# Attention value products in plain float32 for all batches, and four units of block 1 among block 0's output layer

## The chip, the core and the metric

The kernel runs on one core of one Trainium2 chip. A core has a matrix engine (TensorE, PE in the profile; PEld is its weight load), a vector engine (VectorE, DVE), a scalar engine (ScalarE, ACT), GpSimd (POOL) and a queue engine (SyncE, SP) that issues most of the DMAs. The metric is device time of the whole program in microseconds (us), less is better.

## What is computed

Three layers follow each other. The first is attention over 8 batches, 8 heads, 576 tokens and head size 64, with keys and values averaged over groups of 8 tokens, so that each query sees 72 keys:

```
k_p = k.reshape(B, H, Sp, pool, D).mean(axis=3)      # Sp = 72
v_p = v.reshape(B, H, Sp, pool, D).mean(axis=3)
attn = softmax(q @ k_p^T / sqrt(D))
x = attn @ v_p                                       # to 4608 tokens x 512
h = max(max(x @ w1, x @ w2), x @ w3)                 # 512 -> 768
y = h @ w_out                                        # 768 -> 512
out = square(max(y @ w_in2, 0)) @ w_out2             # 512 -> 2048 -> 512
```

All inputs and outputs are float32. The weights come as 64-bit numbers and are converted on the chip.

## The kernel before

The 4608 tokens are taken in 12 blocks of 384. A batch has 576 tokens, so it gives one piece of 384 and one of 192 to the blocks. For each block there are first the attention pieces, then 22 steps on PE: 18 groups of twelve matmuls for the three products x @ w1, w2, w3 (`ps` at L513; six units `f`, three experts each), and 4 groups of eighteen matmuls for the output layer (`ps` at L532). Results of the blocks go to DRAM (`y_dram`), and after all blocks a second part of the program (`moe2_in`, `moe2_out`) does the last layer.

Products of the two MoE layers need float32 accuracy. Each operand is split into a high part in the type fp32r and the remainder, also fp32r (`split`, `split_to` at L133 and L134: a copy on ACT that rounds, a subtraction on DVE or POOL), and three of the four partial products are summed in PSUM (`PARTS`). The alternative is a matmul on plain float32 tiles.

An attention unit (`attend`) is one pair of heads (p of 4) in one piece. It has: `load` (DMAs of k, q, v), `prepare` (pooled k into `kbd`), `softmax` (pooled v into `vst`, scores `sc` at L353, row maximum, exponentials, sums, division on POOL), `transpose` (probabilities `ss` into `tr` in PSUM and from there into `pt` in SBUF) and `values` (the products of `pt` with `vst`, into `x`, which is then an operand of L513). For batch 0 (`whole`, b < NATURAL) `pt` and the pooled values `vst_f` are plain float32 tiles, the two heads are summed into one PSUM bank `av` by two matmuls (L398), and `x` is split from that bank. For batches 1 to 7, `pt` is split into high and low part (L384, L385), `vst` too (L209, L210), each head has its own bank (`av0`, `av1`) and two matmuls (L409, L410) that leave the parts in two halves of the bank's rows; these are summed through `xf` (a copy on ACT, L412, and an addition on DVE, L413), and `x` is split from `xf`.

The order is made in two steps. Every piece of work gets a time in steps (`todo`, sorted in `run`): block j's matmul groups stand at j * 22 and after, attention for a block a number of steps ahead of it (LEAD and LAG numbers), the loads of weights at the start. Then a scheduler of the compiler moves instructions within engines by its own simulation. For block 1, the first `AHEAD` units (three groups each) are put among the four groups of block 0's output layer, at equal distances; their `h` tiles lie in a pool of their own, `ah_p`, since block 0 still holds the six tiles of `h_p`. In the opening, the 18 weight tiles of w1, w2, w3 and then the six of w_out (`wo1`) are loaded (`load_raw`), converted (two instructions each on ACT and DVE, `convert`) and split (ACT and POOL, L133 and L134). Their raw form lies in four buffers that they share with the loads of k and v (`place`).

Of the kernel before, what the change touches and what calls it, by code (L numbers as in the profile page):

```python
# [20 lines left out]
P = 128  # L21
# [42 lines left out]
AHEAD = 2  # L64
# [18 lines left out]
def as_f32(ap):  # L83
    return ap.bitcast(F32)
# [8 lines left out]
def attention_moe_kernel(ctx: ExitStack, tc: tile.TileContext, q, k, v, vn, w1, w2, w3, wo1, wi2, wo2, out):  # L93
# [95 lines left out]
    xf_p = s_at.enter_context(tc.tile_pool(name="xf_p", bufs=1, side="right"))  # L189
# [6 lines left out]
    vst = kv_p.tile([SP, NPAIR, 4, D], F32R, name="vst")  # L196

    kbd = kv_p.tile([P, NPAIR, 2, SP], F32, name="kbd")
    nc.gpsimd.memset(kbd, 0.0)
    vst_f = []  # L200
    for _ in range(2):
        vf = t_p.tile([P, T1], F32, tag="ys", name="vst_f")[:SP].rearrange("s (p a d) -> s p a d", a=3, d=D)
        nc.gpsimd.memset(vf, 0.0)
        vst_f.append(vf)
    K_SCALE = 1.0 / (POOL * D**0.5)
    V_SCALE = 1.0 / POOL

    def split_scaled(hi, lo, src, scale):
        nc.scalar.activation(hi, src, AF.Copy, scale=scale)  # L209
        nc.vector.scalar_tensor_tensor(  # L210
            out=lo, in0=src, scalar=scale, in1=as_f32(hi), op0=ALU.mult, op1=ALU.subtract
        )
# [27 lines left out]
    def prepare_v(p, vr):  # L240
        vs = sm_p.tile([SP, 2, D], F32, tag="vs", name="vs", bufs=2)
        nc.vector.tensor_reduce(out=vs, in_=vr, axis=AX.X, op=ALU.add)
        split_scaled(vst[:, p, 0:4:3], vst[:, p, 1:3], vs, V_SCALE)
# [14 lines left out]
    def pool_v(tiles):  # L258
# [8 lines left out]
        for h in range(2):  # L267
            vh = vp.rearrange("s (p h d) -> s h p d", h=2, d=D)[:, h]
            for i in range(2):
                nc.scalar.activation(vst_f[i][:, :, 2 * h], vh[:, 2 * i : 2 * i + 2], AF.Copy, scale=V_SCALE)  # L270
# [48 lines left out]
    def attend(j, b, s0, n, p, t):  # L319

        kr, vr, qr, pt, sms = [], [], [], [], []
        first, whole = s0 == 0, b < NATURAL
# [47 lines left out]
        def transpose():  # L370
            if whole:
                pt.append(pt_p.tile([SP, 2, T1], F32, tag="pt", name="pt"))
            else:
                pt.append(pt_p.tile([SP, 2, 2, T1], F32R, tag="pt", name="pt"))
            for h in range(2):
# [6 lines left out]
                if not whole:  # L382
                    hi, lo = pt[0][:, 0, h, :n], pt[0][:, 1, h, :n]
                    nc.scalar.activation(hi, tr, AF.Copy)  # L384
                    nc.vector.tensor_tensor(out=lo, in0=tr, in1=as_f32(hi), op=ALU.subtract)  # L385
                elif h:
# [4 lines left out]
        def values():  # L391
# [3 lines left out]
            if whole:  # L395
                av = av_ps.tile([P, T1], F32, tag="av0", name="av0")[:, :n]
                for h in range(2):
                    nc.tensor.matmul(  # L398
                        av, lhsT=vst_f[p // 2][:, p % 2, h : h + 2].rearrange("p a d -> p (a d)"), rhs=pt[0][:, h, :n],
                        start=(h == 0), stop=(h == 1),  # L400
                    )
                split(x, av)
                return
            hi, lo = pt[0][:, 0, :, :n], pt[0][:, 1, :, :n]
            xf = xf_p.tile([P, T1], F32, tag="xf", name="xf")[:, :n]
            for h in range(2):
                av = av_ps.tile([P, T1], F32, tag=f"av{h}", name=f"av{h}")[:, :n]
                lhsT = vst[:, p, 2 * h : 2 * h + 2].rearrange("p a d -> p (a d)")
                nc.tensor.matmul(av, lhsT=lhsT, rhs=hi[:, h], start=True, stop=False)  # L409
                nc.tensor.matmul(av, lhsT=lhsT, rhs=lo[:, h], start=False, stop=True)  # L410
                r, o = slice(h * D, (h + 1) * D), slice((1 - h) * D, (2 - h) * D)
                nc.scalar.activation(xf[r], av[o], AF.Copy)  # L412
                nc.vector.tensor_tensor(out=xf[r], in0=av[r], in1=xf[r], op=ALU.add)  # L413
            split(x, xf)
# [458 lines left out]
```

## Time and profile before

| | |
|---|---|
| time, median of 3 runs (lowest to highest) | 1467.43 us (1466.56 to 1469.72) |
| profiled execution: time, span | 1465.84 us, 1464.0 us |
| PE busy | 1432.9 us, 98% of the span |
| DVE, ACT, POOL busy | 984.6, 763.9, 182.2 us |
| mean granted TensorE clock | 0.993 |

The time of an execution is a little longer than the span from the first to the last instruction. Busy time of PE contains pipelined matmuls whose ends are modelled. In timelines and groups, a float32 matmul is recorded as two instructions, an fp32r one as one; the rows of the program's order, further down, count each matmul once.

### The profile page before, as it was taken

The page shows a single profiled execution, that of the slowest core. Times are in us where ns is not written, and L with a number is a line of the kernel's source. Part 1 is how long each engine was busy: PE and PEld are TensorE (multiplying, and loading weights), DVE is VectorE, ACT ScalarE, POOL GpSimd, SP SyncE. Part 2 cuts the span into 40 slices and gives each one's busy share as a digit, 9 for nine tenths or more (in the row PEclk, how much of TensorE's full clock was granted, in tenths as well). Part 3 has the DMA queues.
Part 4 walks back from the last instruction along what each step waited for, and adds up shares of the span by engine and source line. Part 5 has one row for each costly group of instructions (what it writes and reads, how often), then busy time and mean ns, then how long its engine had stood idle before and what let it go on. Part 6 is the DMA issues. An engine that isn't in the chain of part 4 may idle for free.

```text
span 1464.0 us, 27554 instructions
## 1 busy us (share of the span) xinstructions
PE 1432.9 (98%) x10410; PEld 1409.8 (96%) x10410; DVE 984.6 (67%) x1778; ACT 763.9 (52%) x1983; POOL 182.2 (12%) x228
## 2 busy tenths in 40 slices
PE   6989999999999999999999999999999999999998
PEld 4879999999999999999999999999999999999998
DVE  5896466766765856656426768687776768686765
ACT  7794366655665646655314535353444445454443
POOL 3451012222222212222000000000000000000000
PEclk9899999999999999999999999999999999999999
DMA  7553135443355434422539856666666666565746
GB/s 225 185 168 110 53 115 173 141 134 123 120 164 176 126 124 130 130 101 79 187 116 370 290 196 212 220 210 224 229 231 225 227 216 214 198 245 174 274 144 229
DMA packets 118307, 263.94 MB, mean 180 GB/s; under 512 B 12672, under 2 KB 62848, under 8 KB 118176
## 3 DMA queue, kind: packets, MB, share of 16 engines
q1 hardware_dynamic: 111264, 252.75, 51.0%
q10 hardware_dynamic: 6912, 9.44, 1.8%
q8 instruction: 82, 1.34, 0.4%
q14 instruction: 49, 0.40, 0.1%
HBM read 213.91 MB, written 48.23 MB: 179 GB/s over the span
## 4 chain that ended last, share of the span: by engine, by line
PE 88%; DMA 5%; ACT 3%; DVE 2%; issue 1%; POOL 0%; SPq 0%; DVEq 0%; ACTq 0%; POOLq 0%
PE ps L513 28%; PE ps L673 23%; PE ps L532 10%; PE accB L797 6%; PE accA L797 6%; DMA wo2s<-wo_dram 4%; PE accF L797 3%; PE accE L797 3%; PE sc L353 2%; PE accD L797 2%; PE tr L381 2%; PE av L410 1%; PE av L409 1%; ACT ss L358 1%; DVE wbits L165 1%
## 5 line engine op out<-in xcount | busy, mean ns | idle before, releaser
L513 PE MATMUL ps<-x,w 128*128 128x384 f32 x2592 | 495.7, 342 | 3.3 <-ACT w L133 1.2
L513 PEld LDWEIGHTS ps<-x,w 128*128 128x128 f32 x2592 | 452.0, 190 | 6.1 <-ACT w L133 2.6
L673 PE MATMUL ps<-y,wi2s 128*128 128x256 f32 x3024 | 371.8, 277 | 0.5 <-DVE c L644 0.2
L673 PEld LDWEIGHTS ps<-y,wi2s 128*128 128x128 f32 x3024 | 356.6, 188 | 1.9 <-DVE c L644 0.8
L532 PE MATMUL ps<-h,wo 128*128 128x384 f32 x864 | 162.1, 339 | 3.2 <-POOL wo L134 2.4
L532 PEld LDWEIGHTS ps<-h,wo 128*128 128x128 f32 x864 | 149.5, 189 | 4.0 <-POOL wo L134 2.8
L686 ACT ACTIVATE c<-c 128x512 f32<-128x512 f32 x90 | 56.3, 627 | 167.2 <-DVE c L644 166.6
L644 DVE TENSOR_TENSOR c<-ps,c 128x512 f32<-128x512 f32 x144 | 98.2, 687 | 66.0 <-PE ps L673 64.5
L521 DVE TENSOR_TENSOR hm<-ps,hm 128x384 f32<-128x384 f32 x144 | 79.5, 552 | 72.3 <-PE ps L513 69.9
L133 ACT ACTIVATE g<-c 128x512 fp32r<-128x512 f32 x144 | 90.2, 626 | 56.7 <-DVE c L683 23.3
L797 PE MATMUL accA<-wo2s,g 128*128 128x256 f32 x864 | 115.8, 277 | 0.0
L797 PE MATMUL accB<-wo2s,g 128*128 128x256 f32 x864 | 110.9, 277 | 2.6 <-DMA wo2s<-wo_dram 1.9
L134 DVE TENSOR_TENSOR g<-c,g 128x512 fp32r<-128x512 f32 x144 | 97.6, 685 | 16.2 <-ACT g L133 16.2
L797 PEld LDWEIGHTS accA<-wo2s,g 128*128 128x128 f32 x864 | 107.1, 188 | 0.0
L358 ACT ACTIVATE ss<-sc,st 128x72 f32<-128x72 f32 (+1 forms) x320 | 97.9, 319 | 17.6 <-DVE st L355 15.4
L797 PEld LDWEIGHTS accB<-wo2s,g 128*128 128x128 f32 x864 | 103.9, 188 | 3.2 <-ACT o L766 1.6
L364 POOL TENSOR_TENSOR ss<-ss,st 128x432 f32<-128x432 f32 (+1 forms) x64 | 56.4, 882 | 265.7 <-DVE st L363 182.9
L413 DVE TENSOR_TENSOR xf<-av,xf 64x192 f32<-64x192 f32 (+1 forms) x112 | 50.7, 453 | 46.7 <-ACT xf L412 44.8
L385 DVE TENSOR_TENSOR pt<-tr,pt 72x192 fp32r<-72x192 f32 (+1 forms) x112 | 49.3, 449 | 41.4 <-ACT pt L384 40.1
L412 ACT ACTIVATE xf<-av 64x192 f32<-64x192 f32 (+1 forms) x112 | 45.4, 405 | 54.5 <-PE av L410 40.4
L133 ACT ACTIVATE h<-hm 128x384 fp32r<-128x384 f32 x72 | 37.7, 523 | 64.2 <-DVE hm L521 63.9
L358 ACT ACTIVATION_READ_ACCUMULATOR ss<-sc,st 128x1 f32 (+1 forms) x320 | 65.8, 206 | 0.0
(104 smaller groups left out, 1951.4 us busy)
## 6 DMA issues: line engine op xcount, KB each, us to landing
wo2s<-wo_dram SPq DMA_DIRECT2D x252, 512.0 KB, 5.7
wi2s<-wi_dram SPq DMA_DIRECT2D x24, 512.0 KB, 9.1
wraw<-in_wo_dram SPq DMA_DIRECT2D x22, 512.0 KB, 3.7
wraw<-in_w_dram SPq DMA_DIRECT2D x18, 512.0 KB, 3.4
y_dram<-ys ACTq DMA_DIRECT2D x48, 192.0 KB, 2.0
wraw<-in_wi_dram SPq DMA_DIRECT2D x16, 512.0 KB, 3.5
wi_dram<-wraw SPq DMA_DIRECT2D x16, 512.0 KB, 3.7
wo_dram<-wraw SPq DMA_DIRECT2D x64, 128.0 KB, 2.0
```

Source lines behind the costliest of these rows:

```text
L133: nc.scalar.activation(hi, src, AF.Copy)
L134: engine.tensor_tensor(out=lo, in0=src, in1=as_f32(hi), op=ALU.subtract)
L358: nc.scalar.activation(ss[:, i, h], src[:, i, h], AF.Exp, bias=st[:, 0, i, h : h + 1], accum_out=st[:, 1, i, h : h + 1],)
L364: nc.gpsimd.tensor_tensor(out=ss, in0=ss, in1=st[:, 2].rearrange("p g (h o) -> p g h o", o=1).to_broadcast([m, g, 2, SP]), op=ALU.mult,)
L413: nc.vector.tensor_tensor(out=xf[r], in0=av[r], in1=xf[r], op=ALU.add)
L513: nc.tensor.matmul(ps, lhsT=w1_t[f, e][:, a, kk * P : (kk + 1) * P], rhs=x[kk][:, c], start=(n == 0), stop=(n == 3 * KD - 1),)
L521: nc.vector.tensor_tensor(out=hm, in0=ps, in1=hm, op=ALU.max)
L532: nc.tensor.matmul(ps, lhsT=wo1_t[kk][:, a, d * P : (d + 1) * P], rhs=hs[kk][:, c], start=(n == 0), stop=(n == 3 * KF1 - 1),)
L644: nc.vector.tensor_tensor(out=out, in0=in0, in1=in1, op=ALU.add)
L673: nc.tensor.matmul(bank[:, u * HT : (u + 1) * HT], lhsT=wi2_t[2 * gr + u][i][:, a, o + kk * P : o + (kk + 1) * P], rhs=y_t[j][m][:, c, kk] ...
L686: nc.scalar.activation(c, c, AF.Relu)
L797: nc.tensor.matmul(bank[:, i * 256 : (i + 1) * 256], lhsT=g[:, a, u * HT + i * P : u * HT + (i + 1) * P], rhs=w[:, u, c], start=(n == 0 an ...
```

## The change

`AHEAD` goes from 2 to 4, and the pool `ah_p` with it has four tiles. The path for batches 1 to 7 is taken out of `transpose` and `values`, and all batches go the way that batch 0 went: `pt` is one float32 tile, filled for one head by ACT and for the other by DVE; two float32 matmuls (now L377) sum both heads into `av0`; `x` is split from there. `vst` is one float32 tile with three slots a pair (values of head 0, zeros, values of head 1), cleared once, for all batches; batch 0 had two tiles `vst_f` of its own for it. The pool `xf_p` and the function `split_scaled` go.

```diff
--- before.py
+++ after.py
@@ -61,7 +61,7 @@
 
 LEAD_SECOND = 5
 
-AHEAD = 2
+AHEAD = 4
 BRISK = 0.7
 
 SECOND = (2, NB1 - 1)
@@ -186,30 +186,18 @@
     raw_p = s_at.enter_context(tc.tile_pool(name="raw_p", bufs=4, side="right"))
     sm_p = s_at.enter_context(tc.tile_pool(name="sm_p", bufs=4, side="right"))
     pt_p = s_at.enter_context(tc.tile_pool(name="pt_p", bufs=2, side="right"))
-    xf_p = s_at.enter_context(tc.tile_pool(name="xf_p", bufs=1, side="right"))
     ah_p = s_at.enter_context(tc.tile_pool(name="ah_p", bufs=AHEAD, side="right"))
     sc_ps = s_at.enter_context(tc.tile_pool(name="sc_ps", bufs=2, space=PSUM))
     tr_ps = s_at.enter_context(tc.tile_pool(name="tr_ps", bufs=1, space=PSUM))
     av_ps = s_at.enter_context(tc.tile_pool(name="av_ps", bufs=1, space=PSUM))
 
 
-    vst = kv_p.tile([SP, NPAIR, 4, D], F32R, name="vst")
-
     kbd = kv_p.tile([P, NPAIR, 2, SP], F32, name="kbd")
     nc.gpsimd.memset(kbd, 0.0)
-    vst_f = []
-    for _ in range(2):
-        vf = t_p.tile([P, T1], F32, tag="ys", name="vst_f")[:SP].rearrange("s (p a d) -> s p a d", a=3, d=D)
-        nc.gpsimd.memset(vf, 0.0)
-        vst_f.append(vf)
+    vst = kv_p.tile([SP, NPAIR, 3, D], F32, name="vst")
+    nc.gpsimd.memset(vst, 0.0)
     K_SCALE = 1.0 / (POOL * D**0.5)
     V_SCALE = 1.0 / POOL
-
-    def split_scaled(hi, lo, src, scale):
-        nc.scalar.activation(hi, src, AF.Copy, scale=scale)
-        nc.vector.scalar_tensor_tensor(
-            out=lo, in0=src, scalar=scale, in1=as_f32(hi), op0=ALU.mult, op1=ALU.subtract
-        )
 
 
     spare = [f"spare{i}" for i in range(KF1)]
@@ -240,7 +228,7 @@
     def prepare_v(p, vr):
         vs = sm_p.tile([SP, 2, D], F32, tag="vs", name="vs", bufs=2)
         nc.vector.tensor_reduce(out=vs, in_=vr, axis=AX.X, op=ALU.add)
-        split_scaled(vst[:, p, 0:4:3], vst[:, p, 1:3], vs, V_SCALE)
+        nc.scalar.activation(vst[:, p, 0:3:2], vs, AF.Copy, scale=V_SCALE)
 
     def load_natural(b):
 
@@ -266,8 +254,7 @@
             )
         for h in range(2):
             vh = vp.rearrange("s (p h d) -> s h p d", h=2, d=D)[:, h]
-            for i in range(2):
-                nc.scalar.activation(vst_f[i][:, :, 2 * h], vh[:, 2 * i : 2 * i + 2], AF.Copy, scale=V_SCALE)
+            nc.scalar.activation(vst[:, :, 2 * h], vh, AF.Copy, scale=V_SCALE)
 
     x_t = {}
 
@@ -319,7 +306,7 @@
     def attend(j, b, s0, n, p, t):
 
         kr, vr, qr, pt, sms = [], [], [], [], []
-        first, whole = s0 == 0, b < NATURAL
+        first = s0 == 0
 
         def load():
             if j == 0:
@@ -368,10 +355,7 @@
             sms.append(ss)
 
         def transpose():
-            if whole:
-                pt.append(pt_p.tile([SP, 2, T1], F32, tag="pt", name="pt"))
-            else:
-                pt.append(pt_p.tile([SP, 2, 2, T1], F32R, tag="pt", name="pt"))
+            pt.append(pt_p.tile([SP, 2, T1], F32, tag="pt", name="pt"))
             for h in range(2):
                 if h:
                     tr = av_ps.tile([P, T1], F32, tag="av1", name="tr")[:SP, :n]
@@ -379,11 +363,7 @@
                     tr = tr_ps.tile([SP, T1], F32, tag="tr", name="tr")[:, :n]
                 for i, (c, _) in enumerate(tiles):
                     nc.tensor.transpose(tr[:, c : c + m], sms[0][:, i, h], ident[:m, :m])
-                if not whole:
-                    hi, lo = pt[0][:, 0, h, :n], pt[0][:, 1, h, :n]
-                    nc.scalar.activation(hi, tr, AF.Copy)
-                    nc.vector.tensor_tensor(out=lo, in0=tr, in1=as_f32(hi), op=ALU.subtract)
-                elif h:
+                if h:
                     nc.vector.tensor_copy(pt[0][:, h, :n], tr)
                 else:
                     nc.scalar.activation(pt[0][:, h, :n], tr, AF.Copy)
@@ -392,26 +372,13 @@
             if t == 0:
                 x_t[j][p] = x_p.tile([P, 2, T1], F32R, tag="x", name="x")
             x = x_t[j][p][:, :, t : t + n]
-            if whole:
-                av = av_ps.tile([P, T1], F32, tag="av0", name="av0")[:, :n]
-                for h in range(2):
-                    nc.tensor.matmul(
-                        av, lhsT=vst_f[p // 2][:, p % 2, h : h + 2].rearrange("p a d -> p (a d)"), rhs=pt[0][:, h, :n],
-                        start=(h == 0), stop=(h == 1),
-                    )
-                split(x, av)
-                return
-            hi, lo = pt[0][:, 0, :, :n], pt[0][:, 1, :, :n]
-            xf = xf_p.tile([P, T1], F32, tag="xf", name="xf")[:, :n]
+            av = av_ps.tile([P, T1], F32, tag="av0", name="av0")[:, :n]
             for h in range(2):
-                av = av_ps.tile([P, T1], F32, tag=f"av{h}", name=f"av{h}")[:, :n]
-                lhsT = vst[:, p, 2 * h : 2 * h + 2].rearrange("p a d -> p (a d)")
-                nc.tensor.matmul(av, lhsT=lhsT, rhs=hi[:, h], start=True, stop=False)
-                nc.tensor.matmul(av, lhsT=lhsT, rhs=lo[:, h], start=False, stop=True)
-                r, o = slice(h * D, (h + 1) * D), slice((1 - h) * D, (2 - h) * D)
-                nc.scalar.activation(xf[r], av[o], AF.Copy)
-                nc.vector.tensor_tensor(out=xf[r], in0=av[r], in1=xf[r], op=ALU.add)
-            split(x, xf)
+                nc.tensor.matmul(
+                    av, lhsT=vst[:, p, h : h + 2].rearrange("p a d -> p (a d)"), rhs=pt[0][:, h, :n],
+                    start=(h == 0), stop=(h == 1),
+                )
+            split(x, av)
 
         return load, prepare, softmax, transpose, values
 
```

What follows are rows of the program's order on one engine, first before, then after. On PE, at the end of block 0: `ps<-h,wo_k` are the output layer's products with the k-th tile of w_out (three matmuls each of the first group), `ps<-x,w_0_e` are products of block 1's first unit, `av` and `tr` attention. Before, fourteen matmuls of block 1 stand ahead of these rows and behind the first `ps<-h,wo_0`:

```order
L532 MATMUL ps<-h,wo_1_937 128x384
L513 MATMUL ps<-x,w_0_0_360 128x384 x2
L513 MATMUL ps<-x,w_0_1_376 128x384 x2
L532 MATMUL ps<-h,wo_2_958 128x384 x2
L409 MATMUL av_1454<-pt,vst 128x384
L410 MATMUL av_1454<-pt,vst 128x384
L381 MATMUL tr<-ident,ss 72x128 x3
L513 MATMUL ps<-x,w_0_0_360 128x384
L513 MATMUL ps<-x,w_0_1_376 128x384
L381 MATMUL tr<-ident,ss 72x128 x3
L532 MATMUL ps<-h,wo_2_958 128x384
L532 MATMUL ps<-h,wo_3_997 128x384 x3
```

And after, from block 1's first matmul on:

```order
L480 MATMUL ps<-x,w_0_0_352 128x384 x12
L377 MATMUL av_1489<-pt,vst 128x384 x2
L499 MATMUL ps<-h,wo_1_903 128x384 x2
L480 MATMUL ps<-x,w_0_1_368 128x384 x12
L499 MATMUL ps<-h,wo_1_903 128x384
L499 MATMUL ps<-h,wo_2_922 128x384 x2
L365 MATMUL tr<-ident,ss 72x128
L499 MATMUL ps<-h,wo_2_922 128x384
L499 MATMUL ps<-h,wo_3_953 128x384 x2
L480 MATMUL ps<-x,w_0_2_380 128x384 x4
L499 MATMUL ps<-h,wo_3_953 128x384
```

Ahead of the last product with tile wo_3 there were twenty matmuls of block 1's first unit, of two experts in turn; now there are 28, of three.

On PE, one unit of 384 tokens late in block 1 (transposes, then values), before:

```order
L381 MATMUL tr<-ident,ss 72x128 x6
L513 MATMUL ps<-x,w_5_1_805 128x384 x12
L409 MATMUL av_1781<-pt,vst 128x384
L410 MATMUL av_1781<-pt,vst 128x384
L513 MATMUL ps<-x,w_5_2_846 128x384 x12
L532 MATMUL ps<-h,wo_0_898 128x384 x2
L409 MATMUL av_1786<-pt,vst 128x384
L410 MATMUL av_1786<-pt,vst 128x384
```

And after:

```order
L365 MATMUL tr<-ident,ss 72x128 x6
L480 MATMUL ps<-x,w_5_1_790 128x384 x12
L377 MATMUL av_1693<-pt,vst 128x384 x2
L480 MATMUL ps<-x,w_5_2_823 128x384 x12
L499 MATMUL ps<-h,wo_0_872 128x384 x3
```

The four matmuls of a unit, in two pairs with other work between, have become two float32 ones in one place.

On ACT, in the opening, the write of batch 1's pooled values for the first pair into `vst` (`kbd` is pooled k, `x` the split of an attention product, `wraw`, `wbits` and `w1` the conversion of weights), before:

```order
L238 ACTIVATE kbd_184<-ks_539 64x72 x2
L133 ACTIVATE w1_0_2_388<-wbits_391 128x512
L133 ACTIVATE x_321<-av0_322 128x384
L160 ACTIVATE wbits_414<-wraw_412 128x512
L238 ACTIVATE kbd_184<-ks_597 64x72 x2
L209 ACTIVATE vst_183<-vs_617 72x2x64
L358 ACTIVATE ss_438,st_441<-sc_437,st_441 96x72 x3
```

And after:

```order
L160 ACTIVATE wbits_470<-wraw_468 128x512
L161 ACTIVATE wraw_468<-wraw_468 128x512
L345 ACTIVATE ss_668,st_671<-sc_667,st_671 96x72 x4
L133 ACTIVATE x_535<-av0_536 128x192
L369 ACTIVATE pt_564<-tr_565 72x192
L231 ACTIVATE vst_182<-vs_609 72x2x64
L160 ACTIVATE wbits_486<-wraw_484 128x512
```

The write has gone from its place behind the pooled keys to a later one, behind the split of the same pair's `x` for batch 0.

## Rows read from the trace of the kernel before

**Rows 1.** The page, part 1: busy time of PE and its weight loads.
```profile
PE 1432.9 (98%) x10410; PEld 1409.8 (96%) x10410; DVE 984.6 (67%) x1778; ACT 763.9 (52%) x1983; POOL 182.2 (12%) x228
```

**Rows 2.** Busy time by stretch: length, PE, PEld, DVE, ACT, POOL, granted clock, DMA, GB/s.
```profile
60.00:80.00 20.00, 17.86 (x111) 16.75 (x110) 18.13 (x37) 15.92 (x50) 10.09 (x9) 1.00 0.56 180
80.00:100.00 20.00, 18.07 (x97) 16.89 (x97) 19.37 (x34) 18.10 (x57) 10.45 (x9) 0.91 0.60 187
100.00:120.00 20.00, 16.75 (x94) 15.74 (x93) 17.74 (x28) 14.62 (x48) 11.30 (x8) 0.91 0.37 111
120.00:743.00 623.00, 622.51 (x3777) 618.08 (x3776) 382.90 (x798) 347.57 (x1103) 129.33 (x176) 1.00 0.39 126
743.00:1464.00 721.00, 711.75 (x6137) 707.82 (x6136) 506.98 (x802) 322.89 (x556) 0.00 (x0) 1.00 0.65 226
```

**Rows 3.** The chain of waits inside 120 to 743 us, by line.
```profile
by line: PE ps L513 65.0%; PE ps L532 21.2%; PE sc L353 4.5%; PE tr L381 3.9%; PE av L410 2.3%; PE av L409 2.2%; ACT ss L358 0.5%; ACT pt L384 0.2%; ACT xf L412 0.1%; ACT hm L519 0.1%; ACT x L133 0.0%; issue 0.0%
```

**Rows 4.** PE's waits, 60 to 125 us: total us, times, longest.
```profile
PE av L409 <- DVE xf L413: 1.2, 2, 0.8
...
PE tr L381 <- DVE xf L413: 0.4, 1, 0.4
```

**Rows 5.** Groups of PE instructions, whole span: count, busy us, mean ns.
```profile
L409 PE MATMUL av<-pt,vst 72*128 72x384 f32 x56 | 20.3, 362 | 0.0
...
L409 PE MATMUL av<-pt,vst 72*128 72x192 f32 x56 | 15.2, 272 | 1.2 <-DVE xf L413 1.2
L398 PE MATMUL av<-pt,vst_f 72*128 72x384 f32 x16 | 7.9, 631 | 1.4 <-DVE x L134 1.4
```

**Rows 6.** Timeline of PE around two fp32r products: start, us, instruction.
```profile
306.46 0.34 PE L409 MATMUL av<-pt,vst 72*128 72x384 f32 x1
306.64 0.34 PE L410 MATMUL av<-pt,vst 72*128 72x384 f32 x1
306.81 1.40 PE L513 MATMUL ps<-x,w 128*128 128x384 f32 x7
...
642.62 0.25 PE L409 MATMUL av<-pt,vst 72*128 72x192 f32 x1
...
642.82 3.48 PE L532 MATMUL ps<-h,wo 128*128 128x384 f32 x19
```

**Rows 7.** Timeline of PE around two float32 products of batch 0.
```profile
16.95 1.46 PE L398 MATMUL av<-pt,vst_f 72*128 72x384 f32 x4
18.57 0.39 PE L353 MATMUL sc<-kbd,kq 128*128 128x144 f32 x1 [0.17 <-ACT ss L358]
...
64.10 0.82 PE L398 MATMUL av<-pt,vst_f 72*128 72x192 f32 x4
64.75 0.49 PE L381 MATMUL tr<-ident,ss 96*72 96x96 f32 x4
```

**Rows 8.** Groups of the opening, 0 to 112 us: evictions of the attention products.
```profile
L413 DVE TENSOR_TENSOR xf<-av,xf 64x192 f32<-64x192 f32 x8 | 2.8, 352 | 0.2
L385 DVE TENSOR_TENSOR pt<-tr,pt 72x192 fp32r<-72x192 f32 x8 | 2.7, 344 | 0.1
L412 ACT ACTIVATE xf<-av 64x192 f32<-64x192 f32 x8 | 2.6, 325 | 0.6 <-PE av L410 0.4
...
L384 ACT ACTIVATE pt<-tr 72x192 fp32r<-72x192 f32 x8 | 2.3, 315 | 0.0
...
L134 DVE TENSOR_TENSOR x<-xf,x 128x192 fp32r<-128x192 f32 x4 | 1.9, 483 | 0.0
...
L134 DVE TENSOR_TENSOR x<-av,x 128x192 fp32r<-128x192 f32 x4 | 1.3, 332 | 0.0
...
L210 DVE SCALAR_TENSOR_TENSOR vst<-vs,vst 72x128 fp32r<-72x128 f32 x4 | 1.1, 274 | 0.0
```

**Rows 9.** Timeline of PE at the fourth output weight tile.
```profile
108.04 0.77 PE L532 MATMUL ps<-h,wo 128*128 128x384 f32 x3
111.25 0.69 PE L532 MATMUL ps<-h,wo 128*128 128x384 f32 x1 [2.44 <-POOL wo L134]
```

## The prediction

> **What bounds the kernel now.** I read the page's busy shares first: TensorE (PE) is busy 98% of the span [rows 1]. Such a share mixes stages, so the next view is PE's busy time by stretch [rows 2]. The reader is to see three stages. From 120 us to 743 us, PE is busy 622.51 of 623.00 us at granted clock 1.00, that is at 2.4 GHz: there is no hole in which more matmul time could hide. From 743 us on the second MoE layer runs, which the diff does not touch and whose order of instructions stays the same to the end; I carry it over unchanged. Before 120 us, PE has holes and its clock sinks to 0.91 as a mean over 20 us.
>
> The chain of waits inside 120 to 743 us says the same in another way [rows 3]: 99.1% of it is PE lines, and the evictions that the change removes or halves (L412, L384) hold 0.3%. So the ScalarE (ACT) and VectorE (DVE) work taken away there is worth nothing by itself, and PE time added there is paid in full.
>
> In the opening PE waits for converted weights [rows 9] and for the attention chain [rows 4]. Its holes from 60 to 120 us are 2.14, 1.93 and 3.25 us, and the lowered clock takes 18.07 x 0.09 = 1.6 us and 16.75 x 0.09 = 1.5 us more [rows 2]. Together 10.4 us: that is all that a better opening can give back, since the products of batch 0, which the change leaves as they are, go on until 64.10 us [rows 7].
>
> **The value products.** A unit is one pair of heads over 384 or 192 tokens. Batches 1 to 7 have 28 units of each size (56 L409 matmuls of each size, two per unit) [rows 5]. A unit before is four fp32r matmuls. In the saturated stretch one head of 384 takes 306.81 - 306.46 = 0.35 us from its start to the next instruction's, one head of 192 takes 642.82 - 642.62 = 0.20 us [rows 6]. So 0.70 and 0.40 us a unit.
>
> After, a unit is two float32 matmuls. What those cost is shown by batch 0, which is computed so already: its eight products of 384 are recorded as 16 instructions, two each [rows 5]. Four such instructions of 192 columns, one unit, take 64.75 - 64.10 = 0.65 us, in a stretch at clock 1.00 [rows 2, 7]. Of 384 columns the four that begin at 16.95 us are recorded with 1.46 us, and the engine is idle before its next start [rows 7]. That holds one tail: an fp32r instruction is recorded with 0.34 us but lets the next begin after about 0.175 us [rows 6], so the tail is 0.16 us, and 1.46 - 0.16 = 1.30 us is the unit.
>
> So a 384 unit costs 1.30 - 0.70 = 0.60 us more and a 192 unit 0.65 - 0.40 = 0.25 us more: 28 x 0.60 + 28 x 0.25 = 16.8 + 7.0 = 23.8 us of PE time. Fewer instructions in the program, more time on the engine.
>
> The passage from a float32 product to the fp32r one behind it occurs at up to 56 new places. If it bared the tail each time it would cost 56 x 0.165 = 9.2 us; the same passage stands behind each score and transpose group already, in a stretch with half a microsecond of idle time in all, so I take 0 and keep 9.2 us for the range. A gain from it is excluded: a new change of mode cannot end sooner than none.
>
> A rule of the Trainium skill bears on the size. The page "FP8 and Floating Point Precision", section "TensorE Precision Notes", says that a true float32 product goes through the array in four passes. Taken at the fp32r instruction's own pace this would be an estimate of 4 x 0.175 = 0.70 us a product of 384 and 4 x 0.10 = 0.40 us of 192, in all 28 x 0.70 + 28 x 0.40 = 30.8 us. The trace agrees with the rule in kind, with 0.65 and 0.325 us; the sum goes by the trace.
>
> **The evictions.** A unit loses two ACT copies and two DVE adds into xf, one ACT and one DVE instruction of the split of pt, and a DVE subtraction for vst. From 120 us on that frees engines that wait for PE anyway: nothing. Up to 112 us it counts, since DVE and ACT convert the weights there. DVE: eight adds (2.8 us), half of eight subtractions of pt (1.4 us), four of vst (1.1 us), four splits of x that read av in place of xf, about 0.15 us each (483 ns against 332 ns of batch 0) [rows 8], 0.6 us, and with the first 384 units about 0.8 us: 6.7 us. ACT: eight copies (2.6 us), half of the pt copies (1.2 us), about 1 us for 384 units: near 5 us [rows 8].
>
> **The opening.** PE's largest wait there is for the fourth output weight tile: the instruction at 108.04 us is followed by one at 111.25 us, 2.44 us idle [rows 9]. Two things shrink it. The weights are ready some 5 us earlier, by the relief of ACT and DVE. And with four units of block 1 in the pool, the new order puts 28 matmuls of block 1 ahead of that wait in place of 20, which is 8 x 0.174 = 1.4 us of cover. Eight more stand between the fourth's and the fifth's products, where four stood. When the wait goes, so does the lowered clock behind it. That is the 4.8 us of the stretch 100 to 120 us. Of the 5.7 us of 60 to 100 us I give back the 1.2 + 0.4 us that PE waited for adds of xf [rows 4], and leave the rest, because it is waiting for weights whose loads the change does not hasten. 4.8 + 1.6 = 6.4, say 6 us. Ends: nothing, and all 10.4 us.
>
> The price on the other side: vst is now one tile for all batches. Batch 1's V can be written for a pair only when batch 0's last product of that pair has read it, where it had its own tiles before. On ACT the four writes stand some 30 rows later, behind the split of x of the same pair, and the loads of V stay longer in the four buffers that the weights share. One weight tile that comes late costs PE 2.44 us in the row of the fourth output tile [rows 9]; two such turns, 5 us, are the end that I keep. I take 0, as the writes wait for nothing that ACT has not waited for already.
>
> The remaining edits (one memset for two, one copy of pooled V for two, a smaller pt and vst, two more h tiles) cost under 1 us at the start, beside the first loads.
>
> Sum: 23.8 - 6 = 17.8 us. The profiled execution took 1465.84 us, which gives 1483.6; the median of the runs is 1467.43, 1.6 us higher, which gives 1485. I forecast **1485 us**.
>
> **The rivals.**
> - *Nothing comes back.* The conversions keep their pace, because GpSimd's halves of the split and the loads set it. For it: PE's longest wait, 2.44 us, is for a GpSimd tile [rows 9]. Against: DVE is busy 18.13, 19.37 and 17.74 of each 20 us there, the most of the three engines that convert [rows 2], and its relief is 6.7 us. 1467.4 + 23.8 = 1491 us; with bared tails up to 1500.
> - *All of it comes back*, 10.4 us: 1481 us, and with the 0.9% of the chain of 120 to 743 us that is not PE, 5.6 us, 1475 us.
> - *A slower opening.* The shared vst holds weight buffers: 1467.4 + 23.8 + 3 to 5 = 1494 to 1496 us.
> - *Four passes at the fp32r pace*: 30.8 - 6 = 24.8, 1492 us. The rows of batch 0 speak against it.
> - *The other side: the float32 instruction is as quick as an fp32r one.* Place: the value products after 120 us. Batch 0's products ran in the opening, where the clock moves; if each of the two halves took 0.175 us in a dense stretch, a unit of 384 would cost 0.70 us as before and the opening's 6 us would be the whole effect: 1461 us. It decides from the point where the 56 units cost less than 6 us together, 0.11 us each. Against it: the four instructions of 192 in 0.65 us, in a stretch at clock 1.00 [rows 2, 7], where four fp32r ones take 0.40 us.
>
> **How the numbers follow.** A measurement here tells 0.2%, about 3 us, from no change. Chances: forecast (1480 to 1489) 0.55; nothing back 0.18; all back 0.12; slower opening 0.06; four passes 0.04; the other side 0.05, of which 0.02 falls within 0.2%. Faster 0.03, same 0.02, slower 0.95. The range from 1477 to 1494 leaves out the last part of the second rival, bared tails, the worst opening, and the other side.
>
> **What would show it.** In the profile after, the value products should be 256 float32 instructions (now 224 fp32r and 32 float32), with 0.325 and 0.16 us from start to start; PE should stay full from the opening's end, and the second layer should begin about 18 us later. The second layer should last 721 us as now. The wait for the fourth output tile should be gone or under 1 us. The prediction is wrong if PE has idle time after 120 us, if the opening loses what it lost, or if a 384 unit costs other than 1.3 us.

## The result: 20 us slower, as forecast, and the profile after

The changed kernel takes 1487.18 us (median of 4 runs, 1484.75 to 1488.75) against 1466.99 us of the kernel before in the same comparison (4 runs, 1466.37 to 1469.72). The ratio is 1.0133, with a 95% interval of 1.0112 to 1.0153: slower by 20 us, where 1485 us was forecast, between 1477 and 1494. The profiled execution took 1484.75 us with a span of 1483.0 us.

The page's part 1 and the group of the value products, of the kernel after (group: count | busy us, mean ns | idle before). They answer to [rows 1] and [rows 5].

```profile
PE 1451.0 (98%) x10410; PEld 1415.3 (95%) x10410; DVE 901.5 (61%) x1582; ACT 698.9 (47%) x1813; POOL 175.9 (12%) x227
...
L377 PE MATMUL av<-pt,vst 72*128 72x384 f32 (+1 forms) x256 | 75.2, 413 | 3.8 <-DVE x L134 3.8
```

DVE lost 83 us of work and ACT 65 us, PE gained 18 us, and the time followed PE. The count of PE instructions is 10410 in both, since each float32 matmul is recorded as two: 256 on L377 stand where 224 fp32r and 32 float32 records stood. PE's busy share is 98% in both kernels; it told nothing of the direction.

The stretches of the kernel after, with the columns of [rows 2]:

```profile
60.00:80.00 20.00, 19.18 (x118) 18.05 (x117) 17.57 (x32) 16.33 (x50) 9.75 (x7) 1.00 0.54 170
80.00:100.00 20.00, 17.61 (x92) 16.16 (x91) 16.95 (x28) 17.61 (x60) 11.12 (x8) 0.91 0.53 178
100.00:120.00 20.00, 19.79 (x114) 18.33 (x113) 16.87 (x27) 12.33 (x34) 10.54 (x6) 1.00 0.48 140
120.00:762.00 642.00, 641.12 (x3773) 624.33 (x3772) 305.77 (x617) 286.44 (x949) 121.94 (x176) 1.00 0.38 122
762.00:1483.00 721.00, 710.51 (x6116) 706.11 (x6114) 505.84 (x800) 322.81 (x556) 0.00 (x0) 1.00 0.65 226
```

The opening is fuller: idle time of PE from 60 to 120 us is 0.82 + 2.39 + 0.21 = 3.4 us where it was 7.3 us [rows 2], and of the two lowered stretches one is left. From 120 us to 762 us (721 us before the end, as in [rows 2]) PE is busy 641.12 of 642.00 us, with 77 us less of DVE and 61 us less of ACT than in the stretch that [rows 2] has; the 0.88 us without work are one wait, shown next.

Three pieces of PE's timeline after (start, us, instruction, idle before it in brackets). The first holds units in the full stretch, the second the fourth output weight tile of [rows 9], the third a new wait:

```profile
312.98 1.45 PE L377 MATMUL av<-pt,vst 72*128 72x384 f32 x4
313.97 2.54 PE L480 MATMUL ps<-x,w 128*128 128x384 f32 x12
316.36 0.90 PE L340 MATMUL sc<-kbd,qr 128*128 128x144 f32 x6
...
114.03 0.45 PE L499 MATMUL ps<-h,wo 128*128 128x384 f32 x1 [0.21 <-POOL wo L134]
...
123.68 1.48 PE L480 MATMUL ps<-x,w 128*128 128x384 f32 x7 [0.88 <-ACT ys L505]
```

A unit of 384 is 1.30 us here too, but not from its start to the next one's start, which is 313.97 - 312.98 = 0.99 us. The fp32r product behind it is recorded as beginning while the last float32 half still runs: the twelve on L480 fill 316.36 - 313.97 = 2.39 us, and twelve at 0.173 us take 2.08. The missing 0.31 us stands there. The wait for POOL's half of an output tile fell from 2.44 us to 0.21 us (in a second profile, below, 1.3 us in two waits, the longest 1.03 us). A new one, 0.88 us, is that of a PSUM bank for its eviction into `ys` (L505).

Where the first stage ends is best read from the first instruction of the second layer. The kernel before:

```profile
745.76 12.64 PE L532 MATMUL ps<-h,wo 128*128 128x384 f32 x72
758.24 3.97 PE L673 MATMUL ps<-y,wi2s 128*128 128x256 f32 x31
```

and the kernel after:

```profile
761.04 12.64 PE L499 MATMUL ps<-h,wo 128*128 128x384 f32 x72
773.52 2.67 PE L640 MATMUL ps<-y,wi2s 128*128 128x256 f32 x22
```

So of the 19.0 us by which the span grew, 15.3 us are the first stage, and 3.7 us the second layer (705.8 to 709.5 us), in which the change has no part. (The prediction put the border at 743 us, inside the last output group.)

**An account of lost time.** To see what a few us are made of, I give each PE instruction the time that it takes in a dense row: 0.1733 us an fp32r product of 384 columns, 0.127 a recorded half of a score, 0.1125 or 0.09 one of a transpose, 0.43 one of the ten halves that pool batch 0's values, 0.175 and 0.10 an fp32r value product, 0.324 and 0.165 a recorded half of a float32 one. These are taken from start-to-start times in the full stretches. Their sum up to a moment is the work; the time on the clock minus the work is what was lost by then to waits, to a lowered clock, or to whatever makes an instruction longer than in a dense row. The table is worked out from the traces, one profiled execution each; the experiments are described below.

| kernel | work before the second layer | lost by 60 us | by 120 | by 165 | by 690 | second layer starts | and lasts |
|---|---|---|---|---|---|---|---|
| before | 715.5 | 25.5 | 38.7 | 38.9 | 42.6 | 758.2 | 705.8 |
| after | 739.5 | 25.2 | 32.3 | 33.6 | 34.0 | 773.5 | 709.5 |
| after, second profile | 739.5 | 23.5 | 30.3 | 31.9 | 32.3 | 771.9 | 712.0 |
| AHEAD 2 | 739.5 | 24.6 | 31.1 | 31.4 | 31.7 | 771.3 | 712.0 |
| AHEAD 2, second profile | 739.5 | 25.2 | 32.1 | 34.3 | 34.7 | 774.2 | 711.5 |
| after, float32 doubled | 794.3 | 25.9 | 34.0 | 34.0 | 34.8 | 829.3 | 710.5 |
| batch 1 only | 719.0 | 26.9 | 34.0 | 34.1 | 38.3 | 757.3 | 713.9 |
| before without xf | 715.5 | 24.6 | 36.0 | 36.2 | 39.8 | 755.4 | 712.1 |
| before, fp32r doubled | 746.3 | 26.5 | 39.1 | 39.3 | 43.4 | 789.9 | 712.3 |
| vst of its own for batch 0 | 739.5 | 27.2 | 35.3 | 35.4 | 35.7 | 775.4 | 712.7 |
| single fp32r | 694.5 | 25.3 | 40.9 | 42.0 | 43.3 | 737.9 | 712.3 |
| single fp32r but batch 0 | 700.1 | 24.7 | 30.0 | 32.0 | 33.4 | 733.5 | 709.7 |

By these prices the change adds 24.0 us of work (23.8 predicted) and takes 8.6 us of loss away (6 predicted): 5.3 us in the opening (by 165 us), and 3.3 us between 165 and 690 us, where 3.7 us were lost before and 0.4 us are lost after.

### The profile page after: what moved, and what is told of

Same layout as the page of the kernel before. It is cut to its first block, busy times and chain, and to the rows that moved or that the text cites. A ratio compares the mean times of both kernels' runs of the same rounds, so it can differ in the third digit from the quotient of the medians.

```text
span 1483.0 us, 27227 instructions
## 1 busy us (share of the span) xinstructions
PE 1451.0 (98%) x10410; PEld 1415.3 (95%) x10410; DVE 901.5 (61%) x1582; ACT 698.9 (47%) x1813; POOL 175.9 (12%) x227
## 4 chain that ended last, share of the span: by engine, by line
PE 87%; DMA 7%; DVE 3%; ACT 2%; issue 1%; SPq 0%; DVEq 0%; ACTq 0%
PE ps L480 27%; PE ps L640 22%; PE ps L499 10%; PE accB L764 6%; PE accA L764 6%; PE av L377 3%; DMA wo2s<-wo_dram 3%; PE accE L764 3%; PE accF L764 3%; PE sc L340 2%; PE accD L764 2%; PE tr L365 2%; DMA wraw<-in_w_dram 2%; DMA vr<-in_v_dram 1%; DMA wraw<-in_wo_dram 1%
## 5 line engine op out<-in xcount | busy, mean ns | idle before, releaser
L480 PE MATMUL ps<-x,w 128*128 128x384 f32 x2592 | 495.1, 343 | 3.2 <-ACT w L133 1.5
L480 PEld LDWEIGHTS ps<-x,w 128*128 128x128 f32 x2592 | 450.8, 189 | 11.7 <-ACT w L133 2.4
L488 DVE TENSOR_TENSOR hm<-ps,hm 128x384 f32<-128x384 f32 x144 | 79.9, 555 | 118.5 <-PE ps L480 118.1
L377 PE MATMUL av<-pt,vst 72*128 72x384 f32 (+1 forms) x256 | 75.2, 413 | 3.8 <-DVE x L134 3.8
L134 DVE TENSOR_TENSOR h<-hm,h 128x384 fp32r<-128x384 f32 x72 | 49.8, 692 | 37.3 <-ACT h L133 37.2
L486 ACT ACTIVATE hm<-ps 128x384 f32<-128x384 f32 x72 | 35.3, 490 | 60.7 <-PE ps L480 58.9
```

Source lines behind the costliest of these rows:

```text
L134: engine.tensor_tensor(out=lo, in0=src, in1=as_f32(hi), op=ALU.subtract)
L377: nc.tensor.matmul(av, lhsT=vst[:, p, h : h + 2].rearrange("p a d -> p (a d)"), rhs=pt[0][:, h, :n], start=(h == 0), stop=(h == 1),)
L480: nc.tensor.matmul(ps, lhsT=w1_t[f, e][:, a, kk * P : (kk + 1) * P], rhs=x[kk][:, c], start=(n == 0), stop=(n == 3 * KD - 1),)
L488: nc.vector.tensor_tensor(out=hm, in0=ps, in1=hm, op=ALU.max)
```

## The experiments

Two questions came out of the traces. What gives the opening back its 5 us: DVE and ACT, freed of work, or the cover of two more units of block 1? And what are the 3.3 us of the full stretch: the evictions, or the fp32r pairs of products themselves? Beside these stand the price of a product and the shared vst, on which rivals of the prediction rest. Six of the ten runs were a single profiled execution; the four others give a ratio.

**What a value product costs.** Doubling the float32 products (in after) and the fp32r products (in before) prices a further set of each kind, without any step of the account.

```diff
-            for h in range(2):
+            for h in (0, 1) * (2 if b >= NATURAL else 1):
                 nc.tensor.matmul(
```

> The changed kernel with the value products of batches 1 to 7 run twice into the same bank (the second pass overwrites the first): 56 units more of float32 products in the full stretch. As predicted (1.30 and 0.65 us a unit): 28 x 1.95 = 54.6 us later start of the second layer, 828.1 us. By the split of the time after into kinds of instructions (1.30 and 0.67): 55.3 us, 828.8 us. If the float32 instruction hides part of its time: under 50 us.

```diff
-                nc.tensor.matmul(av, lhsT=lhsT, rhs=hi[:, h], start=True, stop=False)
-                nc.tensor.matmul(av, lhsT=lhsT, rhs=lo[:, h], start=False, stop=True)
+                for _ in range(2):
+                    nc.tensor.matmul(av, lhsT=lhsT, rhs=hi[:, h], start=True, stop=False)
+                    nc.tensor.matmul(av, lhsT=lhsT, rhs=lo[:, h], start=False, stop=True)
```

> The kernel before with the fp32r value products of batches 1 to 7 run twice into the same banks. As predicted (0.70 and 0.40 us a unit): 28 x 1.10 = 30.8 us later start of the second layer, 789.0 us. If an fp32r value product costs more than its start-to-start times in the rows (0.77 and 0.49 us a unit, as the time after divides): 35.4 us, 793.6 us; then the change costs 20 us of PE time and not 23.8.

First instructions of the second layer with doubled float32 products:

```profile
829.34 4.89 PE L640 MATMUL ps<-y,wi2s 128*128 128x256 f32 x39
```

and with doubled fp32r products:

```profile
789.90 4.33 PE L674 MATMUL ps<-y,wi2s 128*128 128x256 f32 x34
```

The first stage grew by 829.34 - 773.52 = 55.8 us (1541.75 us in all) and by 789.90 - 758.24 = 31.7 us (1504.11 us). Over 28 pairs of units that is 1.99 us of float32 for a pair of 384 and 192, and 1.13 us of fp32r; the prediction had 1.95 and 1.10. Both came out within 1.3 us of the predicted prices, and their difference, 24.1 us, is what a second set of float32 products costs over a second set of fp32r ones. The other expectation of the doubled fp32r run, 793.6 us, did not come. Float32 as quick as fp32r (the other side) would have given the two the same step. The Trainium skill's rule of four passes ("FP8 and Floating Point Precision", section "TensorE Precision Notes"), taken at the fp32r pace as the prediction did, would make the first step an estimate of 28 x 4 x (0.35 + 0.20) = 61.6 us; the measured 55.8 us decide against that size.

A doubled unit, in the kernel with float32 products doubled:

```profile
333.17 2.74 PE L377 MATMUL av<-pt,vst 72*128 72x384 f32 x8
335.45 2.58 PE L480 MATMUL ps<-x,w 128*128 128x384 f32 x12
```

From its start to the next start it takes 2.28 us, against 0.99 us of the single one above: 1.29 us for the second pair of products, with no tail in the way.

A second set stands behind a first one, so doubling leaves out what the first one costs at its place among other products. The rows show that too. Two places of the kernel before in the full stretch, each with twelve fp32r products behind it:

```profile
191.38 0.34 PE L409 MATMUL av<-pt,vst 72*128 72x384 f32 x1
191.56 0.34 PE L410 MATMUL av<-pt,vst 72*128 72x384 f32 x1
191.74 2.27 PE L513 MATMUL ps<-x,w 128*128 128x384 f32 x12
193.84 0.41 PE L353 MATMUL sc<-kbd,qr 128*128 128x144 f32 x2
...
238.11 0.25 PE L409 MATMUL av<-pt,vst 72*128 72x192 f32 x1
238.20 0.27 PE L410 MATMUL av<-pt,vst 72*128 72x192 f32 x1
238.31 2.27 PE L513 MATMUL ps<-x,w 128*128 128x384 f32 x12
240.42 0.65 PE L353 MATMUL sc<-kbd,qr 128*96 128x144 f32 x4
```

From the pair's start to the instruction behind the twelve it is 193.84 - 191.38 = 2.46 us and 240.42 - 238.11 = 2.31 us. Twelve products take 2.08 us, so the pairs took 0.38 and 0.23 us, not the 0.35 and 0.20 us that lie between a pair's start and the next start: as with float32 above, a part stands in the row behind. The table has the same reading (start to start over the place and the next six products, less six at 0.1733 us) as the median of all places between 165 and 690 us with six such products ahead and seven behind.

| at one place | 384 columns, us (places) | 192 columns, us (places) |
|---|---|---|
| fp32r pair, before | 0.377 (21) | 0.231 (16) |
| fp32r pair, before without xf (below) | 0.377 (23) | 0.231 (12) |
| two fp32r pairs, before doubled | 0.724 (20) | 0.451 (9) |
| fp32r unit without low parts, one place (below) | 0.377 (11) | 0.231 (18) |
| float32 unit, after | 1.296 (6) | 0.656 (20) |

A unit of before has two such pairs, 0.75 and 0.46 us, and one of after costs 1.30 and 0.66 us. So 28 x (1.296 + 0.656 - 0.754 - 0.462) = 20.6 us is what the change costs PE, where the prediction had 23.8; less the 5.3 us of the opening that makes the 15.3 us of the first stage.

**Do the two more units of block 1 matter?** AHEAD back to 2 in the kernel after:

```diff
-AHEAD = 4
+AHEAD = 2
```

> The changed kernel with AHEAD back at 2: float32 value products for all batches, but only two units of block 1 among block 0's output layer. In the profile after, the second layer's first product starts at 773.5 us (758.2 before). Theory A, the opening's return comes from the relief of DVE and ACT, which have weights ready earlier: the second layer starts at 773.5 to 774.5 us, time within 1 us of the changed kernel's. Theory B, it comes from the cover, the additional matmuls of block 1 in front of the output weights: PE waits again for the fourth or a later output tile, 2 us or more, and the second layer starts at 776 to 778 us.

1489.34 us (4 runs, 1486.21 to 1492.94), ratio to before 1.0133 (1.0109 to 1.0158): the same ratio as with four units. The second layer starts at 771.35 us, 2.2 us earlier than in after, which neither theory had. Since that was a profile each, both were looked at once more.

> The changed kernel unchanged, a second profile. It tells how far the place where the second layer starts (773.5 us) and that layer's length (709.5 us; 705.8 to 713.9 in the profiles so far, with the same order of instructions) vary from run to run. If both 2.2 us to AHEAD 2 and the 2 us to the tile of its own are variation of the opening: a start between 771 and 776 us. If the opening repeats: 773 to 774 us.

> The changed kernel with AHEAD 2, a second profile. If four units instead of two cost 2.2 us in the opening: the second layer starts at 771 to 772 us again, and the wait for the eviction of ys at 123 us that the changed kernel shows is absent. If that difference is variation: 773 us or later.

1485.61 us with four units, 1487.4 us with two; second layer at 771.9 and 774.2 us, now the other way round. PE's waits with AHEAD 2, 60 to 125 us (total us, times, longest), in the first profile:

```profile
PE ps L480 <- ACT w L133: 1.8, 1, 1.8
PE ps L480 <- POOL w L134: 0.7, 1, 0.7
PE av L377 <- DVE x L134: 0.5, 1, 0.5
```

and in the second one:

```profile
PE ps L499 <- POOL wo L134: 1.2, 2, 0.9
PE ps L480 <- POOL w L134: 0.7, 1, 0.7
PE tr L365 <- DVE pt L367: 0.7, 2, 0.4
...
```

The same program waits for other things in two executions, and the sum of its opening moves by 2 to 3 us. Within that, four units and two are the same. The long wait for the fourth output tile (2.44 us in [rows 9]) is small or gone with AHEAD 2 as well, so the cover of eight more matmuls isn't what removed it. Both profiles of the changed kernel show the wait for `ys`; here the second:

```profile
121.67 2.35 PE L480 MATMUL ps<-x,w 128*128 128x384 f32 x12 [1.06 <-ACT ys L505]
```

It isn't in the first profile with AHEAD 2, and the second one has a wait of 1.87 us there for an instruction of DVE (`hm`, L488). Nor is it in two other profiles with AHEAD 4 (float32 doubled; a `vst` of its own for batch 0, below), whose order of instructions in the opening is another one. So whether it comes from the four units isn't shown. Four units alone on the kernel before weren't tried.

**Float32 for batch 1 only**, in the kernel before, AHEAD 2, with `xf` in the buffers of `ys`:

```diff
...
+    vst_1 = kv_p.tile([SP, NPAIR, 3, D], F32, name="vst_1")
...
-        first, whole = s0 == 0, b < NATURAL
+        first, whole = s0 == 0, b <= NATURAL
...
-            xf = xf_p.tile([P, T1], F32, tag="xf", name="xf")[:, :n]
+            xf = t_p.tile([P, T1], F32, tag="ys", name="xf")[:, :n]
```

> The kernel before (AHEAD 2), with batch 1 alone taken over to the float32 way, in a tile of its own; batches 2 to 7 stay split. To make room, xf lies in the buffers of ys. Theory A (relief): the opening gives back what it gave after, 4.7 us, and the eight units of batch 1 cost 4 x 0.53 + 4 x 0.18 = 2.8 us (as the trace after has them) or 4 x 0.60 + 4 x 0.25 = 3.4 us (as predicted): the second layer starts at 756.3 to 757 us, 1 to 2 us earlier than before. Theory B (cover): nearly nothing comes back, it starts at 760 to 761 us. A third possibility is that xf in the buffers of ys makes the output layers wait: then it starts later still, with idle time of PE after 120 us.

1470.51 us (12 runs, 1466.15 to 1473.76), ratio 1.0003 (0.9989 to 1.0017): no difference. The second layer starts at 757.3 us, 0.3 us behind the range of theory A and far from that of theory B. Work grows by 719.0 - 715.5 = 3.5 us, and the loss by 120 us falls by 4.7 us. Its stretch from 60 to 80 us:

```profile
60.00:80.00 20.00, 20.00 (x128) 19.71 (x127) 17.48 (x33) 16.61 (x48) 9.70 (x9) 1.00 0.59 178
```

PE has no hole where it had 2.14 us. So one batch gives back 4.8 us by 165 us, as much as all seven within the variation above (4.6 to 7.5 us), and it does so at AHEAD 2. The before of these differences is one profile; the kernel before with doubled fp32r products, in which batch 1 goes the split way too, lost 39.1 us by 120 us against its 38.7. From 165 to 690 us this kernel, which keeps fp32r in six batches, still loses 4.2 us.

**The evictions alone.** The kernel before without the copy and the add into `xf`; x is split from `av`, so the sum of the two halves is left out of the output.

```diff
...
-                nc.scalar.activation(xf[r], av[o], AF.Copy)
-                nc.vector.tensor_tensor(out=xf[r], in0=av[r], in1=xf[r], op=ALU.add)
-            split(x, xf)
+            split(x, av)
```

> The kernel before without the summing of the two halves through xf (the copy on ACT and the addition on DVE of each head are left out, x is split from the second head's bank; so the output is not the reference's). All matmuls stay. Divided by kinds of instructions, the kernel before loses 3.7 us between 165 and 690 us in pieces too small to show as idle time, the changed one 0.4. Theory A, these pieces are waits behind the evictions of the split way: the loss in that stretch falls under 1.5 us, and with some 3 us from the opening the second layer starts at 752 to 753.5 us (758.2 before). Theory B, they come with the fp32r pairs themselves, which stand in two places a unit among other matmuls: the loss stays at 3 to 4 us and the second layer starts at 755 to 756 us.

1469.58 us; the second layer starts at 755.4 us. The loss by 120 us falls by 2.7 us, about half of the opening's relief. From 165 to 690 us 3.6 us are still lost, as in before: theory B. Two rows of that stretch, 165 to 690 us (columns of [rows 2]), before:

```profile
165.00:690.00 525.00, 524.51 (x3204) 520.37 (x3203) 335.67 (x711) 311.74 (x1009) 122.97 (x168) 1.00 0.40 131
```

and without `xf`:

```profile
165.00:690.00 525.00, 524.84 (x3206) 520.70 (x3205) 286.27 (x616) 271.08 (x924) 117.00 (x169) 1.00 0.40 131
```

DVE does 49 us less and ACT 41 us less there, and PE gets through the same number of instructions, within two, in 525 us. The evictions freed in this full stretch were worth nothing, as the prediction had it, and the 3.3 us that the change saves there have another cause. The split of `pt` was left in here; that it isn't the cause either is shown by the version with single fp32r products, which has the evictions of the changed kernel and fp32r places as dear as those of before (0.377 and 0.231 us). Of the 3.7 us that before loses, 0.5 us is one wait that the row above shows (524.51 of 525.00).

**A vst of its own for batch 0**, in the kernel after:

```diff
+    vst_0 = kv_p.tile([SP, NPAIR, 3, D], F32, name="vst_0")
...
-            nc.scalar.activation(vst[:, :, 2 * h], vh, AF.Copy, scale=V_SCALE)
+            nc.scalar.activation(vst_0[:, :, 2 * h], vh, AF.Copy, scale=V_SCALE)
...
+            w = vst if b >= NATURAL else vst_0
```

> The changed kernel (AHEAD 4) with a tile of its own for the pooled values of batch 0, so that batch 1's need not wait for batch 0's last products. If the shared tile slowed the opening (the rival of the prediction): the second layer starts at 772.5 us or earlier (773.5 after). If not: 773 to 774 us.

1489.81 us, second layer at 775.4 us: not earlier than with the shared tile (773.5, 771.9), and later than either case had it. Nothing shows that the shared vst slows the opening; but PE's order in the opening changed with the tile too, from its 103rd recorded matmul on, and a single profile can't tell less than the 2 to 3 us by which two of the same program differ.

**A single fp32r product.** If float32 is what costs, one fp32r product per head, with the low parts of `pt` and `vst` left out of the computation, keeps the fewer evictions and halves the PE time. The kernel after with AHEAD 2 and:

```diff
-    vst = kv_p.tile([SP, NPAIR, 3, D], F32, name="vst")
+    vst = kv_p.tile([SP, NPAIR, 3, D], F32R, name="vst")
...
-            pt.append(pt_p.tile([SP, 2, T1], F32, tag="pt", name="pt"))
+            pt.append(pt_p.tile([SP, 2, T1], F32R, tag="pt", name="pt"))
```

> The changed kernel with AHEAD 2, and pt and vst rounded to fp32r: two fp32r matmuls a unit in place of two float32 ones, the low parts of both operands are left out. The order and the evictions are those of the changed kernel. If a float32 product costs what the rows say, 1.30 and 0.66 us a unit against 0.35 and 0.20: 28 x (0.95 + 0.46) = 39.5 us less, second layer at 732 us (771.4 with AHEAD 2), some us earlier still if batch 0's units, which lose 5.6 us, stood on the path. Time 1488 - 40 = 1448 us. If the evictions or the opening took over as the bound: later than 740 us.

1450.25 us (4 runs, 1447.57 to 1452.22), ratio 0.9869 (0.9834 to 0.9904). The second layer starts at 737.9 us, 5.9 us later than forecast. The loss by 120 us is 40.9 us, 8.6 us more than in after, and 8.7 us are lost between 60 and 80 us alone, where after loses 1.5. PE's waits from 40 to 80 us there:

```profile
PE tr L365 <- DVE pt L367: 5.7, 5, 2.3
PE av L377 <- DVE x L134: 1.8, 3, 0.9
```

PE waits for `tr` to come free, five times for the copy into `pt`. With the shorter products less PE work stands beside this chain; that this is the reason is my reading and isn't shown. Batch 0 then got its float32 products back, in a tile of its own, with the low parts left out in the other batches as here:

```diff
...
-            pt.append(pt_p.tile([SP, 2, T1], F32R, tag="pt", name="pt"))
+            pt.append(pt_p.tile([SP, 2, T1], F32 if b < NATURAL else F32R, tag="pt", name="pt"))
...
+            w = vst if b >= NATURAL else vst_0
```

> As the run with single fp32r products (AHEAD 2, low parts of pt and vst left out), but batch 0 keeps its float32 products in a tile of its own, since that run lost 8.7 us between 60 and 80 us in an opening of another order. If the opening is as with AHEAD 2: second layer at 771.4 - 39.5 = 732 us, time 1444 us. If rounding alone reorders the opening: 737 us or later again, time near 1450 us.

1446.16 us (4 runs, 1442.73 to 1448.67), ratio 0.9842 (0.9804 to 0.9881), second layer at 733.5 us, near the 732 us of an opening as with AHEAD 2. The loss by 120 us is 30.0 us, 10.9 us less than with single products in all batches. Its stretch from 60 to 80 us:

```profile
60.00:80.00 20.00, 20.00 (x125) 19.48 (x124) 17.65 (x32) 16.96 (x53) 11.48 (x9) 1.00 0.58 185
```

The hole is gone with batch 0 put back; its products, a tile of its own and another order of PE's instructions came together, so which of them closed it isn't separated. This is the fastest version, 1.6% under before, but seven of its batches take one rounded part of each operand. Of the versions with all parts none beats before measurably.

## Why the prediction came out

The time and the direction were right, and so was the mechanism: PE's float32 time decides, and the opening gives part of it back. One term was mis-sized, one reason was half wrong, and part of the agreement is luck.

- *What bounds the kernel.* Right. PE is full from 120 us to the second layer in every variant but for single waits (the longest 1.87 us), DVE and ACT time taken from there bought nothing (before without `xf`), and PE time added there was paid in full (both doublings).
- *The value products, 23.8 us.* This is the term that was mis-sized: 20.6 us. Its float32 side was right, 1.30 and 0.66 us a unit (1.30 and 0.65 forecast). Its fp32r side was too low: a unit costs 0.75 and 0.46 us at its two places, not 0.70 and 0.40, since the time from a pair's start to the next start leaves out what stands in the row behind. For 28 units of each size that is 34.0 us, not 30.8. In the account the same 3.3 us are the loss between 165 and 690 us. It isn't evictions (the two runs above). With 384 columns, a second pair adds 0.347 us to 0.377, so 0.03 us belongs to the place; with 192 it adds 0.220 to 0.231, so 0.01 us belongs to the place and the rest to the products. What causes it inside the engine stays open.
- *The passage from float32 to fp32r, 0 of at most 9.2 us.* Right that no tail is bared: the loss after 165 us is 0.4 us with 56 such places. That a gain is excluded was wrong for the exchange as a whole: fp32r pairs that pay for their places went, and float32 ones that don't came, and that gained the 3.3 us.
- *The opening, 6 us.* Right in size: 6.4 us by 120 us, 5.3 us by 165 us (1.3 us went again, 0.88 us of it in the wait for `ys`); over the two profiles of each AHEAD 4.6 to 7.5 us. Half wrong in the reason: the float32 way of batch 1 does it, and the cover by four units does not. The 1.4 us put down to it can't be seen. How much of the rest is weights that are ready earlier and how much the shorter chain from `av` to `x` (leaving out `xf` alone gave 2.7 us) isn't separated.
- *Shared vst, 0 of at most 5 us.* The variant with a tile of its own shows no such cost.
- *The second layer unchanged.* Its order is, but its length was 705.8 to 713.9 us in these profiles, whichever kernel ran, and the profile of before happens to be the shortest. PE waits there for loads of wo2s. Two profiles of one kernel differed by 2.5 us (709.5 and 712.0). The largest of these waits from 758 us on, in the kernel before (total us, times, longest):

```profile
PE accB L797 <- DMA wo2s<-wo_dram: 1.9, 2, 1.5
```

and with AHEAD 2, from 771 us on:

```profile
PE accB L764 <- DMA wo2s<-wo_dram: 4.9, 4, 3.5
```

So the sum was right partly by luck, because two things met: the first stage grew by 15.3 us where 17.8 us were forecast, and the second layer by 3.7 us where none were. The medians differ by 20 us; which part of the 5 us above 15.3 belongs to the change isn't settled, as only profiled executions show the stages.

Of the rivals, nothing back (1491 us) falls with the opening's 5.3 us; all back (1481 us) had 10.4 us, of which half came; four passes and float32 as quick as fp32r fall with the doublings; a slower opening falls with the same 5.3 us, and the variant with two tiles shows nothing for it.

## What to carry to other kernels

Where the matrix engine is full, count its columns and types, not its instructions: two float32 products cost 1.30 us where four fp32r ones took 0.75, and some 150 us less work on the two other engines didn't pay for it. Use the type that spares evictions only where the matrix engine waits for the engines that evict; here one batch in the opening gave back as much as seven. Price a product at its place, over the products behind it, and not by the next start. Before a cause is given for 2 us of an opening, look at the same program twice.

## What the runs showed of the hardware

- A float32 product is recorded as two instructions, and the fp32r product behind it as starting inside the second: after a unit of 384 the next start comes at 0.99 us of 1.30, and the 0.31 us are missing from the row behind. Start-to-start times at a change of type mislead by a quarter; sums over several instructions don't.
- An fp32r pair of 384 columns costs 0.377 us at a place among other products and a further pair behind it 0.347 us; of 192 columns 0.231 and 0.220 us. A float32 unit shows no such extra: 1.296 us at its place, and 1.309 us for the second one behind it.
- The second layer, which the edits leave alone, lasted 705.8 to 713.9 us over twelve profiles, with PE's waits for wo2s loads on accB alone between 0.3 and 5.4 us. Two profiles of the same kernel differed by at most 2.5 us in it.
